# Cosformer attention with a mixture of adapters: the last six slots in three pairs, x of late outputs added by GpSimd, logits ahead of the transposes of x

## The chip, the cores and the metric

The kernel runs on one core of a Trainium2 chip. The metric is device time in microseconds (us) of one execution; lower is better. Times before and after are medians over runs on a chip.

A core has five engines that run side by side, each with its own queue of instructions in program order. TensorE (PE in the profile; PEld is its weight load) multiplies matrices and transposes by multiplying with an identity. VectorE (DVE) and ScalarE (ACT) do elementwise work and can read PSUM, where matmuls write. GpSimd (POOL) does elementwise work in SBUF and here also issues the loads. SyncE (SP) issues the stores. 16 DMA engines move data between the chip's memory and SBUF.

## The reference

Inputs q, k and v have 8 batches, 8 heads, 576 positions and 64 features. A linear attention with cosine weights comes first:

```python
theta = np.pi / 2.0 * pos / S
phi(x) = concat([relu(x) * cos(theta), relu(x) * sin(theta)])     # 128 features
kv  = einsum('bhsf,bhsd->bhfd', phi(k), v)
z   = sum(phi(k), axis=2)
num = einsum('bhsf,bhfd->bhsd', phi(q), kv)
den = einsum('bhsf,bhf->bhs', phi(q), z) + 1e-06
x   = (num / den), heads side by side: 4608 rows of 512
```

Then a mixture of adapters on x, with 8 experts of rank 16, of which each row uses the best two:

```python
logits = x @ w_gate
topk   = the two largest of a row's 8 logits
w      = softmax over these two
out    = x + sum over the two experts e of w[e] * (x @ A[e]) @ B[e]
```

## The kernel before, in words

**Tiles.** The 4608 rows of x are worked in 36 slots of 128 rows, NT in the code. Nine slots serve two batches: slots 0 to 3 of each nine belong to the first, 5 to 8 to the second, and the fifth (numbers 4, 13, 22, 31; `mixed`) holds 64 rows of each. A position is written as r * 9 + s, so a batch has nine columns s of 64 rows, and a slot takes two columns.

**Loads.** k, q and v of each batch come by one load each, nearly all issued by GpSimd, cast to bf16 on the way. Five buffers of each are used in turn: after the last scaling of one batch's k, GpSimd issues the loads of batches further on (`load_k(b + 3)`, `load_q(b + 2)`, `load_v(b + 3)`).

**Attention.** For each batch k is cut at zero and multiplied by cos and sin: `relu_k` on VectorE cuts columns in place and `scale_k` on GpSimd multiplies, two instructions for a column. Of batches 2 to 7, GpSimd does columns 0 to 6 in this way; VectorE does column 7 and ACT column 8, cut and multiplied in one instruction (`scale_k1`). `kv` on TensorE sums phi(k) x v over a batch's nine columns into the two PSUM banks `cd`, with a column of ones beside v for z, and `kv_out` copies the sums to SBUF on ACT. For a slot, `transp_q` transposes q and multiplies it by cos and sin in one matmul against a diagonal (from slot 27 on in 64x64 pieces, line 201; before that line 213), `evac_q` copies it out of PSUM on ACT with the cut at zero, `numden` multiplies it with the sums (lines 247 and 252), and `normalise` on VectorE takes the reciprocal of the denominators (line 259) and writes x to SBUF in bf16 (`xt`, line 266).

**Mixture.** `transp_x` transposes x into PSUM (`xz`, line 274), `evac_x` copies it to SBUF on VectorE (line 280). `logits` multiplies it with all experts' A and with w_gate at once, into a PSUM bank `za` (line 300). Slots are gated in groups that share a bank `za`: `gate_a` (maximum, sum, mask, scale) and `gate_b` (mask times sigmoid, and the product with x @ A, giving `zg`, line 335) run on VectorE, with the sigmoid on ACT in between (`gate_sig`, line 326). `za` has one buffer, so the next group's first logits wait for this group's `zg`. `transp_z` transposes `zg` into the other half of `xz` (line 348), and the next `evac_x` takes it along; at the end `evac_z` copies it alone. Then `delta` makes the output in one PSUM bank with two matmuls: x times the identity (`delta_x`, line 366) and `zg` times all experts' B (`delta_z`, line 371). `evac_o` copies it to SBUF on ACT as f32 (line 382, tile `osb`, 24 buffers) and `store` sends it off on SP. The outputs' banks are the two `cd`, in turn, or, while `kv` holds these, a buffer of `qd` that the q transposes use otherwise.

**Order.** The order on every engine is the order of the program, written by hand. The loop over slots n is, in this order: the copy of x transposed of slot n - 1; `normalise(n)`; q of slot n + 1 (`move_q`); logits that are "early"; some `kv`; the gates; one output or two from the list `todo`; `transp_x(n)`; `transp_z`; VectorE's share of k and the cut; GpSimd's share with the loads behind it; logits that are "late"; `numden(n + 1)`; ACT's share of k. Tables such as `early_at`, `late_at`, `gate_a_at` and `move_at` say at which n each group comes. Stores are held back until k of batch 7 has landed (line 529 and `held`). After the loop the last slots are finished by a sequence written out.

**Groups before.** Slots 0 to 32 form eleven groups of three, 33 and 34 a pair, and 35 a group of its own, with a bank from `qd`. For most groups all three logits are late ones, in the step before the first gate.

Of the kernel before, what the change touches and what calls it, by code (L numbers as in the profile page):

```python
# [13 lines left out]
NS = 9  # L14
# [5 lines left out]
def kernel(ctx, tc, q, k, v, w_gate, A, Bw, out):  # L20
# [255 lines left out]
    def evac_x(n, g=None):  # L276

        c = DCH if g is None else DCH + len(groups[g])
        xT_t[n] = t = p_xt.tile([128, DCH + 3, 128], BF16, name="xT")
        nc.vector.tensor_copy(t[:, 0:c], xz[:, 0:c * 128].rearrange("p (c s) -> p c s", c=c))  # L280
        if g is not None:
            zgT_t[g] = t[:, DCH:]

    groups = [list(range(i, i + 3)) for i in range(0, NT - 3, 3)]
    groups += [[NT - 3, NT - 2], [NT - 1]]
    group_of = {n: g for g, t in enumerate(groups) for n in t}

    def logits(n):
        g = group_of[n]
        i = n - groups[g][0]  # L290
        if i == 0:
            if g == len(groups) - 1:
                t = qd.tile([128, 512], FP32, name="zb", tag="qd")
            else:
                t = ps.tile([128, 512], FP32, name="za")
            za_t[g] = t[:, 0:3 * ZW].rearrange("p (i z) -> p i z", z=ZW)
            u_t[g] = t[:, 3 * ZW:3 * ZW + 3 * E].rearrange("p (i e) -> p i e", e=E)
        xT = xT_t.pop(n)
        for c in range(DCH):
            nc.tensor.matmul(out=za_t[g][:, i, :], lhsT=xT[:, c, :], rhs=AW[:, :, c, :],  # L300
                             start=(c == 0 and i == 0), stop=(c == DCH - 1),
                             skip_group_check=True)
# [36 lines left out]

    def zT_ps(g):  # L340
        n = len(groups[g])
        at = 512 + (256 if g == len(groups) - 1 else 0)
        return xz[:, at:at + n * 128].rearrange("p (c s) -> p c s", c=n)

    def transp_z(g):
        zg = g_t.pop(g)
        for i in range(len(groups[g])):
            nc.tensor.transpose(out=zT_ps(g)[:, i], in_=zg[:, i], identity=ident)
# [25 lines left out]
    def delta(n, own=True):  # L374
        delta_x(n, own)
        delta_z(n)

    def evac_o(n, eng="act"):
        src = osb_t[n]
        osb_t[n] = t = p_o.tile([128, DM], FP32, name="osb")  # L380
        if eng == "act":
            nc.scalar.copy(t, src)  # L382
        else:
            nc.vector.tensor_copy(t, src)
# [15 lines left out]
    def put(at, step, what):  # L400
        at.setdefault(step, []).append(what)
# [5 lines left out]
    kv_at[3] = [(1, s) for s in (5, 4, 7, 8, 6)]  # L407
    for b in range(2, B):
        first = b // 2 * NS + b % 2 * 4
        at = {2: 5, 3: 8, 4: 12, 5: 15, 6: 21, 7: 24}[b]  # L410
        for s0, s1 in ((0, 3), (3, 7)):
            put(relu_at, at, (b, s0, s1))
        for s in range(7):
            put(pool_at, at, (b, s))
        for i in range(2):
            put(dve_at, at, (b, 7, i))
            put(act_at, first - 4 + i, (b, 8, i))
        for ahead, cols in ((2, (7, 0, 1, 2)), (1, (3, 4, 5, 8, 6))):
            for s in cols:
                put(kv_at, first - ahead, (b, s))  # L420

    early_at, late_at, gate_a_at, gate_b_at, move_at = {}, {}, {}, {}, {}
    prev = 5
    for g, t in enumerate(groups[:-2]):
        tight = g > 7
        at = max(t[-1] + (1 if tight else 2), prev + 1)
        if g == 1:
            at += 1  # L430
        for n in t:
            if n + 1 == at:
                put(early_at, at, n)
            else:
# [5 lines left out]
    put(late_at, NT - 2, NT - 3)  # L440

    with tc.manual_schedule():
        for s in range(6):
            make_diag(s)
        wu = qd.tile([128, DM], FP32, name="wu", tag="qd")
        for i in range(24):
            nc.tensor.matmul(out=wu, lhsT=ones, rhs=wide, start=True, stop=True)  # L447
        for s in range(NS):
            scale_k(0, s, ("act" if s < 7 else "dve", "dve"))
            kv(0, s)  # L450
        nc.scalar.activation(warm, halfpi, AF.Sigmoid)
        for s in range(6, NS):
# [23 lines left out]
        def emit(d, own=True, eng="act"):  # L476
            delta(d, own)
            evac_o(d, eng)
            if held is None:
                store(d)  # L480
            else:
                held.append(d)

        for n in range(NT - 1):
            if n > 0:
                g = move_at.get(n - 1, (None,))[0]
                evac_x(n - 1, g)
                if g is not None:
                    todo += groups[g]
            normalise(n)  # L490
# [12 lines left out]
            for g in gate_b_at.get(n, ()):  # L503
                gate_b(g)
            now = todo[:2 if len(todo) > 3 else 1]
            del todo[:len(now)]
            for d in now:
                emit(d, n not in kv_at)
            for g in gate_a_at.get(n, ()):
                gate_sig(g)  # L510
            transp_x(n)
            for g in move_at.get(n, ()):
                transp_z(g)
            for b, s, i in dve_at.get(n, ()):
                scale_k1(b, s, i, "dve")
            for b, s0, s1 in relu_at.get(n, ()):
                relu_k(b, s0, s1)
            for b, s in pool_at.get(n, ()):
                scale_k(b, s)
                if s == 6:  # L520
# [47 lines left out]
_INS = ['q', 'k', 'v', 'moe_w_gate', 'moe_A', 'moe_B']  # L568
_OUTS = [((4608, 512), 'float32')]
# [25 lines left out]
```

## Time and profile before

| | us |
|---|---|
| median of 3 runs | 116.31 |
| lowest to highest | 116.16 to 116.43 |
| profiled execution | 116.59 |
| its span, first to last instruction and transfer | 114.8 |
| busy: TensorE / VectorE / ACT / GpSimd | 97.4 / 81.3 / 77.5 / 59.1 |

The profiled execution has 1.8 us around its span. In rows of single instructions the columns are: start, duration, engine, line, operation, output<-input with shapes, count, and in brackets idle time before it and what ended that. Rows of stages are: stage, its length, then busy time and instructions of PE, PEld, DVE, ACT and POOL, TensorE's granted clock, the DMA engines' busy share and GB/s. Rows of the chain are start, duration, engine, tile and line. Matmuls overlap: their pace is the distance of their starts, not their duration.

### The profile page before, as it was taken

To read this page: it belongs to the slowest core of one execution; us is meant where nothing else is said; L and a number is where in the kernel's file an instruction comes from. 1 tells how busy PE (TensorE), PEld (TensorE's weight loads), DVE (VectorE), ACT (ScalarE), POOL (GpSimd) and SP (SyncE) were. 2 spreads that over 40 slices of the span, in tenths; PEclk is the share of its full clock that TensorE was granted. 3 is DMA by queue.
4 is the path that set the end of the run, shared out by engine and by line. 5 is a ranking of instruction groups with operands and counts; after the bars stand their busy time and mean duration, and the time that the engine had idled before them with its cause. 6 is when DMAs were issued, how large, how long until landed. Compare 5 with 4: busy or idle time off the path is not lost.

```text
span 114.8 us, 5003 instructions
## 1 busy us (share of the span) xinstructions
PE 97.4 (85%) x2087; PEld 74.0 (65%) x2108; DVE 81.3 (71%) x288; ACT 77.5 (68%) x169; POOL 59.1 (51%) x118
## 2 busy tenths in 40 slices
PE   3998686877998999999999999999997998988710
PEld 1347466766876688777788788578786876655200
DVE  5697588559849858799666974996589448696520
ACT  5088579746845947588786964995769486795820
POOL 5991222248999995899996008959900000000000
PEclk9999999999999999999999999999999999999998
DMA  2999999999999999999999999999989335342692
GB/s 41 381 209 206 210 209 206 203 189 210 205 211 206 208 208 208 208 208 208 207 210 206 214 203 242 275 345 375 347 300 360 121 91 183 113 158 106 225 328 90
DMA packets 19670, 24.77 MB, mean 216 GB/s; under 512 B 2624, under 2 KB 14528, under 8 KB 19648
## 3 DMA queue, kind: packets, MB, share of 16 engines
q0 software_dynamic: 13856, 13.84, 72.5%
q1 hardware_dynamic: 5792, 10.62, 26.3%
q8 instruction: 16, 0.26, 0.9%
q14 instruction: 6, 0.05, 0.1%
HBM read 28.85 MB, written 9.44 MB: 334 GB/s over the span
## 4 chain that ended last, share of the span: by engine, by line
PE 45%; DMA 28%; DVE 12%; issue 4%; ACT 3%; POOL 3%; POOLq 0%; ACTq 0%
DMA k<-in_k_dram 14%; DMA v<-in_v_dram 12%; PE cd L180 10%; PE nd L252 6%; PE xz L274 6%; PE za L300 6%; PE qd L213 6%; DVE xt L266 4%; PE dx L366 3%; PE qd L201 2%; PE cd L371 2%; DVE zg L335 2%; DMA out_dram<-osb 2%; DVE xT L280 2%; ACT qpT L229 2%
## 5 line engine op out<-in xcount | busy, mean ns | idle before, releaser
L229 ACT ACTIVATE qpT<-qd 128x512 bf16<-128x512 f32 x71 | 38.6, 596 | 19.5 <-PE qd L213 14.6
L280 DVE COPY xT<-xz 128x512 bf16<-128x512 bf16 (+1 forms) x36 | 17.1, 475 | 13.5 <-PE xz L274 9.0
L266 DVE TENSOR_TENSOR xt<-nd,rden 128x512 bf16<-128x512 f32 x36 | 24.9, 691 | 1.2
L156 POOL TENSOR_SCALAR kp<-k,cos_tab 128x256 bf16<-128x256 bf16 x42 | 20.2, 480 | 10.5 <-PE cd L180 7.0
L180 PE MATMUL cd<-v,kp 64*128 64x128 bf16 x576 | 18.9, 217 | 1.4 <-DMA v<-in_v_dram 1.1
L156 POOL TENSOR_SCALAR kp<-k,sin_tab 128x256 bf16<-128x256 bf16 x42 | 20.0, 476 | 0.0
L274 PEld LDWEIGHTS <-xt 128*128 128x128 bf16 x144 | 10.2, 116 | 14.5 <-DVE xt L266 11.9
L252 PE MATMUL nd<-kvsb,qpT 128*128 128x65 bf16 (+1 forms) x320 | 17.5, 195 | 1.0 <-DVE qpT L231 0.5
L180 PEld LDWEIGHTS <-kp 64*128 64x128 bf16 x576 | 16.3, 94 | 3.1 <-issue 1.1
L274 PE MATMUL xz<-ident,xt 128*128 128x128 bf16 x144 | 14.6, 224 | 4.3 <-DVE xt L266 3.4
L213 PE MATMUL qd<-diag,q 128*64 128x128 bf16 x432 | 17.2, 222 | 0.7 <-DMA q<-in_q_dram 0.7
L213 PEld LDWEIGHTS <-q 128*64 128x64 bf16 x432 | 12.9, 109 | 2.1 <-DMA q<-in_q_dram 0.8
L382 ACT COPY osb<-cd 128x512 f32<-128x512 f32 x23 | 13.4, 594 | 1.2 <-PE cd L371 0.8
L252 PEld LDWEIGHTS <-qpT 128*128 128x128 bf16 (+1 forms) x320 | 12.6, 99 | 2.1 <-ACT qpT L229 0.7
L300 PE MATMUL za<-AW,xT 128*128 128x144 bf16 x140 | 11.4, 226 | 0.5 <-DVE zg L335 0.5
L247 PE MATMUL nd<-eps_hi,ones 128*128 128x4 bf16 x72 | 11.6, 169 | 0.0
L259 DVE RECIPROCAL rden<-nd 128x8 f32<-128x8 f32 x36 | 7.3, 203 | 5.9 <-PE nd L252 5.7
L300 PEld LDWEIGHTS <-xT 128*128 128x128 bf16 x144 | 9.3, 98 | 1.6 <-DVE xT L280 0.6
L62 POOL DMA_DIRECT2D v<-in_v_dram x8 | 6.2, 779 | 5.1 <-DMA q<-in_q_dram 4.3
L382 ACT COPY osb<-dx 128x512 f32<-128x512 f32 x12 | 6.9, 595 | 2.7 <-remote 2.7
L447 PE MATMUL wu<-wide,ones 128*128 128x512 bf16 x24 | 6.7, 448 | 2.0 <-DVE AW L115 2.0
L62 POOL DMA_DIRECT2D q<-in_q_dram x8 | 6.2, 770 | 3.4 <-DMA k<-in_k_dram 3.4
(69 smaller groups left out, 129.6 us busy)
## 6 DMA issues: line engine op xcount, KB each, us to landing
out_dram<-osb SPq DMA_DIRECT2D x32, 256.0 KB, 4.2
v<-in_v_dram POOLq DMA_DIRECT2D x8, 576.0 KB, 17.8
q<-in_q_dram POOLq DMA_DIRECT2D x8, 576.0 KB, 16.5
k<-in_k_dram POOLq DMA_DIRECT2D x7, 576.0 KB, 15.0
k0f<-in_k_dram SPq DMA_DIRECT2D x1, 1152.0 KB, 5.4
out_dram<-osb SPq DMA_DIRECT2D x8, 128.0 KB, 2.9
AW<-in_moe_A_dram POOLq DMA_DIRECT2D x1, 128.0 KB, 18.2
Ball<-in_moe_B_dram POOLq DMA_DIRECT2D x1, 128.0 KB, 16.7
```

Of the source, the lines that this page charges most:

```text
L62: eng.dma_start(out=t, in_=rows(dram, b))
L156: nc.gpsimd.tensor_scalar(out=dst, in0=src, scalar1=tab, scalar2=1.0, op0=ALU.mult, op1=ALU.mult)
L180: nc.tensor.matmul(out=kvz[par][:, g], lhsT=kp_t[b][pr, s, g], rhs=v_rhs(b, g, s, pr), start=(first and g == 0), stop=(last and g == G - 1))
L213: nc.tensor.matmul(out=t[cols, j, 2 * gi:2 * gi + 2, :], lhsT=q_b[b][:, 2 * gp + gi, s, :], rhs=diag[:, s, i], start=(j == 0 and gi == 0), ...
L229: nc.scalar.activation(t, src, AF.Relu)
L247: nc.tensor.matmul(out=nd[:, gg, D:4 * W:W], lhsT=ones, rhs=eps_hi, start=True, stop=False, skip_group_check=True)
L252: nc.tensor.matmul(out=nd[pr, gg, j * W:(j + 1) * W], lhsT=qpT[:, j, pr], rhs=kv_t[b][:, h % 2, h // 2, :], start=False, stop=(j == 3), sk ...
L266: nc.vector.tensor_tensor(out=x, in0=nd[:, :, :, 0:D], in1=rden.rearrange("p (g j) -> p g j", g=2).to_broadcast([128, 2, 4, D]), op=ALU.mult)
L274: nc.tensor.transpose(out=xz[:, c * 128:(c + 1) * 128], in_=x[:, c], identity=ident)
L280: nc.vector.tensor_copy(t[:, 0:c], xz[:, 0:c * 128].rearrange("p (c s) -> p c s", c=c))
L300: nc.tensor.matmul(out=za_t[g][:, i, :], lhsT=xT[:, c, :], rhs=AW[:, :, c, :], start=(c == 0 and i == 0), stop=(c == DCH - 1), skip_group_ ...
L382: nc.scalar.copy(t, src)
```

## The change

Six things change, mostly in the planning of the order.

- Groups: slots 0 to 29 form ten groups of three and 30 to 35 three pairs. All use the bank `za`.
- Placement of groups: the fifth to eighth groups are gated one step earlier, the eleventh too (it has only slots 30 and 31), and logits move from behind `transp_x` to the place ahead of `kv` and of `transp_x` ("early") where the tables allow it. The first logits of a group whose bank is freed only in that step stay late.
- k: GpSimd scales five columns of batch 2, seven of batch 3, eight of batches 4 and 5, and all nine of batches 6 and 7. ACT takes columns 5, 6 and 8 of batch 2 and column 8 of batches 3, 4 and 5; VectorE column 7 of batches 2 and 3. The steps at which GpSimd starts are 5, 8, 12, 17, 20, 23 where they were 5, 8, 12, 15, 21, 24. `kv` takes the columns in another order.
- Loads behind a batch's scaling come after its last column on GpSimd, whichever that is.
- Late outputs: in steps 28 to 34 (seven outputs, 22 to 28) TensorE only multiplies `zg` with B; ACT copies that to SBUF and GpSimd adds x in place (`delta_add`) before the store.
- The end: the second gate of slots 32 and 33 comes right behind the last `normalise`, outputs 33, 34 and 35 come behind the last z transposes, and VectorE copies output 34 where it copied 35.

```diff
-    groups = [list(range(i, i + 3)) for i in range(0, NT - 3, 3)]
-    groups += [[NT - 3, NT - 2], [NT - 1]]
+    groups = [list(range(i, i + 3)) for i in range(0, NT - 6, 3)]
+    groups += [[i, i + 1] for i in range(NT - 6, NT, 2)]
...
+    def delta_add(n, own=True):
+
+        if own:
+            dx = cd[dx_n[0] % 2]
+            dx_n[0] += 1
+        else:
+            dx = qd.tile([128, DM], FP32, name="dx", tag="qd")
+        g = group_of[n]
+        nc.tensor.matmul(out=dx, lhsT=zgT_t[g][:, n - groups[g][0], :], rhs=Ball,
+                         start=True, stop=True)
+        osb_t[n] = dx
+        evac_o(n)
+        t = osb_t[n]
+        nc.gpsimd.tensor_tensor(out=t, in0=t, in1=xt_t.pop(n), op=ALU.add)
...
-        at = {2: 5, 3: 8, 4: 12, 5: 15, 6: 21, 7: 24}[b]
-        for s0, s1 in ((0, 3), (3, 7)):
+        at = {2: 5, 3: 8, 4: 12, 5: 17, 6: 20, 7: 23}[b]
+        n_pool = {2: 5, 3: 7, 4: 8, 5: 8}.get(b, 9)
+        for s0, s1 in ((0, 3), (3, n_pool)):
             put(relu_at, at, (b, s0, s1))
-        for s in range(7):
+        for s in range(n_pool):
             put(pool_at, at, (b, s))
         for i in range(2):
-            put(dve_at, at, (b, 7, i))
-            put(act_at, first - 4 + i, (b, 8, i))
...
+            if n_pool <= 7:
+                put(dve_at, at, (b, 7, i))
+            if n_pool < 9:
+                put(act_at, first - 4 + i, (b, 8, i))
+            if n_pool == 5:
+                put(act_at, first - 3 + i, (b, 6, i))
+                put(act_at, first - 2, (b, 5, i))
...
-    for g, t in enumerate(groups[:-2]):
-        tight = g > 7
-        at = max(t[-1] + (1 if tight else 2), prev + 1)
+    for g, t in enumerate(groups[:-1]):
+        at = max(t[-1] + 1, prev + 1)
         if g == 1:
             at += 1
         for n in t:
-            if n + 1 == at:
-                put(early_at, at, n)
+            if t[-1] + 1 < at or (n < t[-1] and prev == at - 1):
+                put(late_at, at - 1, n)
             else:
-                put(late_at, at - 1, n)
+                put(early_at, max(n + 1, at - 1), n)
...
-                emit(d, n not in kv_at)
+                emit(d, n not in kv_at, add=n > 27)
...
-        evac_x(NT - 2)
+        evac_x(NT - 2, g10)
         normalise(NT - 1)
-        transp_z(g10)
-        logits(NT - 2)
-        evac_z(g10, [("act", 0, 3)])
+        gate_b(g11)
         todo += groups[g10]
-        for d in todo[:-3]:
+        for d in todo[:-1]:
             emit(d)
         transp_x(NT - 1)
-        gate_a(g11)
-        emit(todo[-3])
-        gate_sig(g11)
         evac_x(NT - 1)
+        logits(NT - 2)
+        transp_z(g11)
         logits(NT - 1)
-        gate_b(g11)
-        emit(todo[-2])
+        evac_z(g11, [("act", 0, 2)])
+        emit(todo[-1])
         gate_a(g12)
-        transp_z(g11)
-        evac_z(g11, [("act", 0, 2)])
         gate_sig(g12)
-        emit(todo[-1])
+        emit(NT - 4)
         gate_b(g12)
+        transp_z(g12)
+        evac_z(g12, [("dve", 0, 2)])
         emit(NT - 3)
-        transp_z(g12)
-        evac_z(g12, [("dve", 0, 1)])
-        emit(NT - 2)
-        emit(NT - 1, eng="dve")
+        emit(NT - 2, eng="dve")
+        emit(NT - 1)
```

More of the change, by code (lines that the diff above doesn't have):

```diff
@@ L291, in logits @@
         if i == 0:
[L292 to L295, printed above, removed]
+            t = ps.tile([128, 512], FP32, name="za")
             za_t[g] = t[:, 0:3 * ZW].rearrange("p (i z) -> p i z", z=ZW)
@@ L341, in zT_ps @@
         n = len(groups[g])
-        at = 512 + (256 if g == len(groups) - 1 else 0)
-        return xz[:, at:at + n * 128].rearrange("p (c s) -> p c s", c=n)
+        return xz[:, 512:512 + n * 128].rearrange("p (c s) -> p c s", c=n)
     def transp_z(g):
@@ L409 @@
         first = b // 2 * NS + b % 2 * 4
-        at = {2: 5, 3: 8, 4: 12, 5: 15, 6: 21, 7: 24}[b]
-        for s0, s1 in ((0, 3), (3, 7)):
+        at = {2: 5, 3: 8, 4: 12, 5: 17, 6: 20, 7: 23}[b]
+        n_pool = {2: 5, 3: 7, 4: 8, 5: 8}.get(b, 9)
+        for s0, s1 in ((0, 3), (3, n_pool)):
             put(relu_at, at, (b, s0, s1))
-        for s in range(7):
+        for s in range(n_pool):
             put(pool_at, at, (b, s))
         for i in range(2):
-            put(dve_at, at, (b, 7, i))
-            put(act_at, first - 4 + i, (b, 8, i))
-        for ahead, cols in ((2, (7, 0, 1, 2)), (1, (3, 4, 5, 8, 6))):
-            for s in cols:
-                put(kv_at, first - ahead, (b, s))
+            if n_pool <= 7:
[5 more added lines that the diff above has]
+                put(act_at, first - 2, (b, 5, i))
+        order = (7, 0, 1, 2, 3, 4, 8, 6, 5) if n_pool <= 7 else (0, 1, 2, 3, 4, 5, 8, 6, 7)
+        if n_pool == 9:
+            order = range(NS)
+        for j, s in enumerate(order):
+            put(kv_at, first - (2 if j < 4 else 1), (b, s))
     early_at, late_at, gate_a_at, gate_b_at, move_at = {}, {}, {}, {}, {}
     prev = 5
-    for g, t in enumerate(groups[:-2]):
-        tight = g > 7
-        at = max(t[-1] + (1 if tight else 2), prev + 1)
+    for g, t in enumerate(groups[:-1]):
+        at = max(t[-1] + 1, prev + 1)
         if g == 1:
@@ L474, with emit @@
         first_loads = persist.tile([1, 8], BF16, name="first_loads")
-        def emit(d, own=True, eng="act"):
-            delta(d, own)
-            evac_o(d, eng)
+        def emit(d, own=True, eng="act", add=False):
+            if add:
+                delta_add(d, own)
+            else:
+                delta(d, own)
+                evac_o(d, eng)
             if held is None:
@@ L519 @@
                 scale_k(b, s)
-                if s == 6:
+                if (b, s) == pool_at[n][-1]:
                     if b + 3 < B:
```

1 line of the change is left out of this document (removed).

## The prediction

> **What bounds the kernel now.** I read the page first (engine shares, the slices, the chain), then the chain in order of time, then busy time by stage, then the order of instructions on each engine where stages differ.
>
> ```profile
> PE 97.4 (85%) x2087; PEld 74.0 (65%) x2108; DVE 81.3 (71%) x288; ACT 77.5 (68%) x169; POOL 59.1 (51%) x118
> DMA  2999999999999999999999999999989335342692
> 18.82 15.56 DMA k<-in_k_dram
> 34.90 0.81 DVE k L165 x2
> ...
> 47.36:83.98 36.62, 35.32 (x760) 28.22 (x768) 27.93 (x94) 27.80 (x61) 27.64 (x58) 1.00 1.16 253
> 83.98:101.30 17.32, 16.04 (x452) 12.39 (x455) 12.48 (x43) 12.98 (x28) 0.00 (x0) 1.00 0.55 191
> ```
>
> The chain is a transfer until 34.4 us (18.82 + 15.56): the load of k for batch 3, which VectorE awaits in slot 8. From there nothing waits for loads. Between 47.36 and 83.98 us (slots 13 to 26) TensorE is busy 35.32 of 36.62 us at full clock: it is the bound, with 1.3 us of gaps. From 83.98 to 101.30 GpSimd is idle and TensorE has the same 1.3 us of gaps in half the time.
>
> I count in steps: from the start of TensorE's q transposes for one slot to the next slot's.
>
> ```profile
> 88.17 0.45 PE L201 MATMUL qd<-diag,q 64*64 64x64 bf16 x32
> 91.28 0.45 PE L201 MATMUL qd<-diag,q 64*64 64x64 bf16 x32
> 95.04 0.45 PE L201 MATMUL qd<-diag,q 64*64 64x64 bf16 x32
> ...
> 50.59 0.38 PE L371 MATMUL cd<-Ball,xT 128*128 128x512 bf16 x1
> 50.81 0.39 PE L274 MATMUL xz<-ident,xt 128*128 128x128 bf16 x4
> 51.03 0.17 PE L247 MATMUL nd<-eps_hi,ones 128*128 128x4 bf16 x1
> 51.42 0.64 PE L213 MATMUL qd<-diag,q 128*64 128x128 bf16 x16
> ```
>
> The paces, first from the starts above, then from the chain in order of time:
>
> ```profile
> 52.97 0.17 PE xz L348 x3
> 53.13 0.75 PE za L300 x12
> 54.18 0.57 PE qd L213 x16
> 54.75 1.00 PE cd L180 x32
> 57.86 1.22 PE cd L180 x40
> ```
>
> A matmul of the output pair costs 0.22 us (50.59 to 50.81), the pair 0.43, four x transposes 0.22 (to 51.03), a slot's numerators 0.39 (to 51.42). Three z transposes cost 0.17, one slot's logits 0.25 (0.75 for three), q transposes 0.57 (0.38 from slot 27), kv sums 1.00 for four columns and 1.22 for five.
>
> **The change, part by part.**
>
> *Loads and columns of k.* Batch 2 goes from seven GpSimd columns to five, so 4 scalings fewer at 0.455 apart: its three load issues move from 33.65 to about 31.9.
>
> ```profile
> 33.65 0.79 POOL L62 DMA_DIRECT2D k<-in_k_dram  x1
> 34.81 0.90 DVE L165 TENSOR_SCALAR k<-k 128x768 bf16<-128x768 bf16 x2
> 45.81 0.69 DVE L165 TENSOR_SCALAR k<-k 128x768 bf16<-128x768 bf16 x2
> ```
>
> VectorE's two relus took 0.90 us while GpSimd issued loads, 0.69 while it stood idle, and they are on the chain. The issues will be over by 34.2: **-0.2**. The Trainium skill, "SBUF — State Buffer", § Who interferes with whom, says that VectorE in a two-port mode and GpSimd shut each other out for whole instructions; the rows agree. The transfers start no earlier (the DMA row is full), and the load that is waited for was issued long before. ACT's four scalings more for batch 2 end before the wait for k at 34.4 does. Later issues move too: those after batch 4 by 0.9 (two more scalings), q of batch 7 by two steps, to about 66, still 20 us before slot 31 needs it; the stores on SP wait for k of batch 7, which stays queued behind earlier loads. Eight scalings leave VectorE and four leave ACT (slots 23 to 28); only the one that held up ACT's q copy at 86.80 is ahead of something that waits, and is counted below.
>
> A cost here: batch 6 now has 18 scalings, 8.2 us, begun behind batch 5's sixteen and a load issue, hence about 67.0 to 75.2. The relu of batch 7 comes up on VectorE at about 74.7. By the rows above it may have to wait for the port. If until 75.2, it ends near 75.9, and the x copy behind it, which needs its transposes at 75.8, moves by **+0.1**. Bounds: 0, and 1.3 (the stream, as long as it is, begun 1.2 later).
>
> *Steps 13 to 26.* Groups come one step earlier: TensorE does one output pair (0.43) and one group of z transposes (0.17) more in here. The logits ahead of the x transposes cost the same 0.25 and fill time in which TensorE would wait for x. Slot 14 gets a wait: its logits sit behind the gate of the group before, which frees the bank. Against each step's length before, by these paces: 14 +0.86 (two logits, and 0.36 for the wait); 15 -0.62 (three logits out, one in, a gap of 0.1 gone); 17 and 20 +0.67 each (two logits and z transposes in); 18 -0.33 (three logits and z transposes out, one logit and a pair in, a gap gone); 19 -0.06 (a gap); 21 -0.67 (three logits and z transposes out, one logit in); 23 +0.43 (two logits and z transposes in, less gaps); 24 -0.69 (as 21); 26 +0.17 (z transposes); the others nothing. Together **+0.4**. With no gap filled it is +0.9 (0.43 + 0.17 + 0.3 for the wait), with every gap gone -0.7 (0.6 less 1.3).
>
> *Steps 27 to 34.* Each of the seven late outputs drops its 0.22 us matmul; step 30 emits one output where two were. But two other loops set a floor.
>
> ```profile
> 86.80 1.09 ACT L229 ACTIVATE qpT<-qd 128x512 bf16<-128x512 f32 x2 [0.19 <-ACT kp L151]
> 93.34 0.65 ACT L188 CAST kvsb<-cd 128x260 bf16<-128x260 f32 x2 [0.42 <-PE cd L180]
> 99.93 1.08 ACT L229 ACTIVATE qpT<-qd 128x512 bf16<-128x512 f32 x2 [0.86 <-PE qd L201]
> 101.07 0.30 PE L252 MATMUL nd<-kvsb,qpT 128*128 128x65 bf16 x4
> 101.30 0.45 PE L201 MATMUL qd<-diag,q 64*64 64x64 bf16 x32
> 101.86 1.08 ACT L229 ACTIVATE qpT<-qd 128x512 bf16<-128x512 f32 x2 [0.26 <-PE qd L201]
> ...
> 101.66 0.69 DVE L266 TENSOR_TENSOR xt<-nd,rden 128x512 bf16<-128x512 f32 x1
> 102.47 0.56 DVE L335 TENSOR_TENSOR zg<-za,em 128x384 bf16<-128x384 f32 x1
> 103.08 0.42 PE L300 MATMUL za<-AW,xT 128*128 128x144 bf16 x4 [0.27 <-DVE zg L335]
> 103.85 0.21 DVE L259 RECIPROCAL rden<-nd 128x8 f32<-128x8 f32 x1 [0.50 <-PE nd L252]
> 104.09 0.69 DVE L266 TENSOR_TENSOR xt<-nd,rden 128x512 bf16<-128x512 f32 x1
> ```
>
> First, q transposes to ACT to numerators: 99.93 to 101.86, 1.92 us. Second, a step whose logits wait for the gate of the same step: 101.66 to 104.09, 2.43 us. After: step 27 1.92 (was 1.93); 28 1.92 (was 2.26: ACT's k scaling stood before the q copy at 86.80 and is gone); 29 2.91 (was 3.11); 30 3.28 (was 3.76: 0.66 less work, 0.2 back, since ACT's 0.65 us copy of the kv sums has 0.47 of cover left); 31 2.42 (was 1.92, the wait for the gate); 32 1.93 (was 2.42, one logit later removed); 33 2.50 (was 1.92, the same wait); and to the last reciprocal 2.15 (was 103.85 - 101.30 = 2.55). Sum 19.03 against 19.87: **-0.8**. Step 31 holds up numerators and the next reciprocal behind the logits; that is in the 2.42. Bounds: the dropped matmuls hidden, +0.0; no new wait, -1.4.
>
> *The add.* It isn't on TensorE's path: the output goes PSUM to SBUF on ACT as before and only its store waits. The price isn't in the trace.
>
> ```profile
> 72.42 0.48 POOL L156 TENSOR_SCALAR kp<-k,sin_tab 128x256 bf16<-128x256 bf16 x1
> 72.88 0.48 POOL L156 TENSOR_SCALAR kp<-k,cos_tab 128x256 bf16<-128x256 bf16 x1
> 72.99 0.41 DVE L280 COPY xT<-xz 128x512 bf16<-128x512 bf16 x1
> 100.97 0.42 DVE L280 COPY xT<-xz 128x512 bf16<-128x512 bf16 x1
> ```
>
> A scaling of 256 elements takes 0.48 us. Twice the elements makes 0.93; five times the bytes (two inputs, f32) makes 2.4. I take 1.4, nearer the instruction of the same engine. The cover: adds come one per 2.0 to 3.3 us from about 87.2, and the last store issue comes at 110.0, behind eight store issues of about 0.6 (four took 2.56, quoted below); so the seven adds must end by 105.2, 18.0 us for seven, 2.6 us each. Behind a late add waits SP's whole queue. VectorE's copies from PSUM took 0.41 beside a busy GpSimd and 0.42 beside an idle one, so the adds don't slow them. The Trainium skill, "GPSIMD Engine Reference", § 3.1, gives an add of 2048 f32 as 4497 ns, by which an estimate for 512 is 1.1 us; its § 2.1 adds about 6 us once for the first call of a freshly loaded kernel. No run here shows that yet, and by it the sum would be the same.
>
> *The end.* The final sequence before:
>
> ```profile
> 105.72 0.58 ACT L382 COPY osb<-cd 128x512 f32<-128x512 f32 x1 [0.44 <-DMA out_dram<-osb]
> 106.20 0.19 ACT L326 ACTIVATE za<-tg 128x16 f32<-128x16 f32 x1
> 108.58 2.56 SPq L395 DMA_DIRECT2D out_dram<-osb  x4
> 109.63 0.69 DVE L384 COPY osb<-cd 128x512 f32<-128x512 f32 x1 [0.66 <-PE cd L371]
> ```
>
> (The wait at 105.72 is not for a store: the output's matmuls end just then.) ACT's sigmoid at 106.20 stood behind that copy, then two gates in a row. The change gates slots 32 and 33 in the loop's rhythm, with their sigmoid done before slot 35's x. From the last x (t = 0, 104.09 before): zg at 0.81, x transposes 0.75, x copy 1.20, logits 1.28 and 1.67, gate to 2.75, sigmoid 3.02 (behind one output copy), zg 3.45, z transposes 3.92, z copy 4.23, output 34 at 4.69, output 35 at 5.50 because its bank is output 33's, which now comes behind the z transposes; ACT's copy ends at 6.49 and SP issues the last store at 6.51. Before: 108.58 + 2.56 less one issue of about 0.6, less 104.09: 6.45. **0.0** within 0.1, bounds -0.4 (the bank free in time) and +0.5.
>
> **The sum.** -0.2 + 0.1 + 0.4 - 0.8 + 0.0 = -0.5 us in the profiled execution, 114.8 of span in 116.59; the median of the runs is 116.31, 0.3 below, and the change is taken from that: 115.8.
>
> **Rivals.** (1) The gaps fill better: the +0.4 of steps 13 to 26 vanishes and goes to -0.2, all else as forecast: 115.2. For it: 1.3 us of gaps; against: I could fill few by hand. (2) Nothing measurable: steps 31 and 33 wait 0.2 longer each: 116.2. (3) Slower, by the port: the relu of batch 7 is shut out by GpSimd's stream. It decides from a stall of 0.6 us in all, that is, when batch 6's stream ends after 75.7; with a stall of 1.3, 117.0. For it: the stream is back to back, 0.455 apart with 0.48 each, and batches 5, 6 and 7 now follow without a pause; against: 0.5 us is all that is left of it when the relu comes. (4) The add is dear: at 3.0 us the last stores go 3.0 later, 118.8. Only the byte bound comes near. By the skill's 6 us and 2.4 us an add together, the adds end 4.8 late, 120.6; with 1.4 us they end at 103.0 and cost nothing.
>
> **How the numbers follow.** Forecast 0.50 (115.4 to 116.1), (1) 0.15, (2) 0.10, (3) 0.18, (4) 0.07. A measurement can tell about 0.2%, 0.23 us, from no change. Faster: 0.15 and nearly all of the forecast, 0.62; same: (2) and the forecast's edge, 0.13; slower 0.25. Range 114.9 to 116.8: below, a twentieth; above, (4) and the worse third of (3).
>
> **What would show it.** The relus at slot 8 at 0.69; the q transposes that stand at 83.98 near 0.3 later; 0.8 us less from there to the last reciprocal, with steps 31 and 33 near 2.4 showing TensorE's logits released by zg; relus of batch 7 longer than 0.75 would speak for (3); adds above 2.6 us, or SP waiting for GpSimd after 105, for (4). The prediction is wrong if those q transposes come after 84.7, or if the last x isn't earlier than 104.09.

## The result: 116.89 us, slower by half a per cent

| | before | after |
|---|---|---|
| median, us (9 runs each) | 116.29 | 116.89 |
| lowest to highest | 116.10 to 116.43 | 116.74 to 117.36 |
| profiled execution / its span | 116.59 / 114.8 | 117.36 / 115.6 |

The ratio is 1.0053, with a 95% interval of 1.0037 to 1.0069: slower, by more than the 0.2% that can be told from no change, and 0.1 us above the predicted range (114.9 to 116.8, with 115.8 as the forecast). The execution profiled for the changed kernel was the longest of its nine. A second profile of the same kernel (`after_again`) has 116.71 and a span of 114.9; where the two differ, both are given.

The page of the changed kernel: engine shares, GpSimd's slices, and the new operation's group (busy us, mean ns, idle before it and what ended that).

```profile
PE 100.4 (87%) x2101; PEld 74.4 (64%) x2101; DVE 79.9 (69%) x280; ACT 76.9 (67%) x168; POOL 71.2 (62%) x133
POOL 5992222247988994999179989989910435544000
L387 POOL TENSOR_TENSOR osb<-osb,xt 128x512 f32<-128x512 f32 x7 | 8.1, 1158 | 13.3 <-ACT osb L393 13.3
```

GpSimd now works until 105.6 us. An add takes 1.16 us, and GpSimd waits for ACT before the adds (13.3 us in all). The stages that the prediction used, each from one start of q transposes to another, first of `after`, then of `after_again`:

```profile
47.10:84.98 37.88, 37.16 (x776) 28.69 (x772) 27.28 (x88) 27.77 (x60) 33.07 (x70) 1.00 1.15 255
84.98:102.26 17.28, 15.55 (x448) 11.78 (x445) 12.92 (x45) 12.03 (x27) 6.11 (x6) 1.00 0.45 157
```

```profile
47.04:84.35 37.31, 36.92 (x778) 28.62 (x774) 27.21 (x88) 27.71 (x60) 32.93 (x70) 1.00 1.14 251
84.35:101.62 17.27, 15.54 (x447) 11.77 (x445) 12.91 (x45) 12.01 (x27) 6.10 (x6) 1.00 0.50 175
```

Slot 8, the relus of batch 7 and the end in `after`, on VectorE, TensorE, ACT and SP:

```profile
34.36 0.29 DVE L153 TENSOR_SCALAR kp<-k,cos_tab 128x256 bf16<-128x256 bf16 x1 [1.12 <-DMA k<-in_k_dram]
34.76 0.69 DVE L165 TENSOR_SCALAR k<-k 128x768 bf16<-128x768 bf16 x2
...
74.84 1.28 DVE L165 TENSOR_SCALAR k<-k 128x768 bf16<-128x768 bf16 x2
...
104.62 0.69 DVE L266 TENSOR_TENSOR xt<-nd,rden 128x512 bf16<-128x512 f32 x1
...
108.21 0.42 DVE L332 TENSOR_TENSOR zg<-za,em 128x256 bf16<-128x256 f32 x1
```

```profile
106.41 0.41 PE L297 MATMUL za<-AW,xT 128*128 128x144 bf16 x4
...
108.69 0.28 PE L344 MATMUL xz<-ident,zg 128*128 128x128 bf16 x2 [1.00 <-DVE zg L332]
110.08 0.38 PE L362 MATMUL cd<-xt,ident 128*128 128x512 bf16 x1 [0.24 <-ACT osb L393]
...
110.71 0.59 ACT L393 COPY osb<-cd 128x512 f32<-128x512 f32 x1 [0.68 <-PE cd L367]
...
109.14 2.79 SPq L406 DMA_DIRECT2D out_dram<-osb  x4
```

Term by term, in us. "Undisturbed" sets `after_again` against the profile of before, and in steps 13 to 26 against a kernel that equals the one before up to slot 27 (`b_add`, below), for a reason that the section on the prediction gives.

| term | forecast | profile to profile | undisturbed |
|---|---|---|---|
| slot 8, from k's landing to slot 13's q transposes (43.54 - 34.41; 43.28 - 34.36) | -0.2 | -0.21 | -0.21 |
| steps 13 to 26, relu of batch 7 in it | +0.5 | 37.88 - 36.62 = +1.26 | 37.31 - 36.39 = +0.92 |
| steps 27 to the last x (104.09 - 83.98; 104.62 - 84.98) | -0.8 | 19.64 - 20.11 = -0.47 | -0.47 |
| last x to the end of the span (114.79 - 104.09; 115.56 - 104.62) | 0.0 | 10.94 - 10.70 = +0.24 | +0.24 |
| sum | -0.5 | +0.82 | +0.48 |

By the medians the change made +0.60. The execution of `after_again` in the last column lay 0.18 below the median of its runs.

### The profile page after: what moved, and what is told of

It is laid out like the page before. It is cut to its first block, busy times and chain, and to the rows that moved or that the text cites. A ratio compares the mean times of both kernels' runs of the same rounds, so it can differ in the third digit from the quotient of the medians.

```text
span 115.6 us, 5017 instructions
## 1 busy us (share of the span) xinstructions
PE 100.4 (87%) x2101; PEld 74.4 (64%) x2101; DVE 79.9 (69%) x280; ACT 76.9 (67%) x168; POOL 71.2 (62%) x133
## 4 chain that ended last, share of the span: by engine, by line
PE 49%; DMA 25%; DVE 13%; issue 3%; POOL 3%; ACT 3%; POOLq 0%; ACTq 0%
DMA k<-in_k_dram 14%; DMA v<-in_v_dram 12%; PE cd L180 10%; PE za L297 8%; PE qd L213 7%; PE nd L252 6%; DVE xt L266 5%; PE xz L274 5%; DVE zg L332 3%; PE dx L362 2%; PE cd L362 2%; DVE xT L280 2%; PE cd L367 2%; PE qd L201 2%; PE xz L344 2%
## 5 line engine op out<-in xcount | busy, mean ns | idle before, releaser
L280 DVE COPY xT<-xz 128x512 bf16<-128x512 bf16 (+2 forms) x36 | 17.3, 479 | 15.2 <-PE xz L344 8.3
L156 POOL TENSOR_SCALAR kp<-k,cos_tab 128x256 bf16<-128x256 bf16 x46 | 22.6, 490 | 7.2 <-DVE k L165 6.4
L156 POOL TENSOR_SCALAR kp<-k,sin_tab 128x256 bf16<-128x256 bf16 x46 | 21.9, 476 | 0.0
L387 POOL TENSOR_TENSOR osb<-osb,xt 128x512 f32<-128x512 f32 x7 | 8.1, 1158 | 13.3 <-ACT osb L393 13.3
L393 ACT COPY osb<-cd 128x512 f32<-128x512 f32 x24 | 13.9, 594 | 2.3 <-PE cd L367 2.2
L297 PE MATMUL za<-AW,xT 128*128 128x144 bf16 x144 | 12.8, 227 | 1.0 <-DVE zg L332 0.7
L464 PE MATMUL wu<-wide,ones 128*128 128x512 bf16 x24 | 8.3, 525 | 2.0 <-DVE AW L115 2.0
L393 ACT COPY osb<-dx 128x512 f32<-128x512 f32 x11 | 6.4, 594 | 3.8 <-PE dx L367 3.0
```

Of the source, the lines that this page charges most:

```text
L156: nc.gpsimd.tensor_scalar(out=dst, in0=src, scalar1=tab, scalar2=1.0, op0=ALU.mult, op1=ALU.mult)
```

## Experiments

Three theories for the loss: **A**, the new placement of logits and groups costs; **B**, the pairs and the new end cost; **C**, GpSimd's longer shares of k and VectorE shut each other out. Names with b_ are the kernel before with one part of the change; names with a_ are the changed kernel with one part undone or moved. Each ratio is to the kernel before on the same chip, with its 95% interval.

### One part of the change alone

`b_logits`: the placement.

```diff
-        tight = g > 7
-        at = max(t[-1] + (1 if tight else 2), prev + 1)
+        at = max(t[-1] + 1, prev + 1)
...
-            if n + 1 == at:
-                put(early_at, at, n)
-            else:
+            if t[-1] + 1 < at or (n < t[-1] and prev == at - 1):
                 put(late_at, at - 1, n)
+            else:
+                put(early_at, max(n + 1, at - 1), n)
```

> The kernel before with only the placement of the changed one (logits ahead of kv and of the x transposes, the fifth to eighth groups gated one step earlier), groups, k, add and end as before. Theory A (this placement is what costs: TensorE does more in steps 13 to 26, loses about 0.1 us at each change from logits to kv, ACT gets two outputs and a k scaling in one step): slower by 0.5 to 0.9 us, 116.8 to 117.2, q transposes of slot 28 at 84.5 or later. Theory B (the pairs and the new end cost): within 0.2 of before. Theory C (GpSimd and VectorE block each other because of the longer k share): within 0.2 of before.

Measured: 116.48, ratio 1.0021 (1.0004 to 1.0039). Steps 13 to 26 take 37.28, as long as in the whole change; from there to the last x 19.43 (84.54 to 103.97), 0.7 less than before. Placement costs 0.9 in one stage and has 0.7 back in the next.

`b_end`: groups and end (the groups' lines of the diff shown ahead of the prediction and its part after the loop, nothing else).

```diff
-    groups = [list(range(i, i + 3)) for i in range(0, NT - 3, 3)]
-    groups += [[NT - 3, NT - 2], [NT - 1]]
+    groups = [list(range(i, i + 3)) for i in range(0, NT - 6, 3)]
+    groups += [[i, i + 1] for i in range(NT - 6, NT, 2)]
...
```

> The kernel before with only the groups of two and the sequence after the loop of the changed kernel; placement up to slot 29 as before. Theory A: within 0.2 of before (steps 31 and 33 +0.5 and +0.4, steps 32 and the last -0.9, the end +0.2). Theory B: slower by 0.5 or more, 116.8, of which 0.3 or more behind the last x. Theory C: as A.

Measured: 116.64, ratio 1.0037 (1.0024 to 1.0051). From slot 28's q transposes to the last x 20.24 (+0.13), from there to the end 10.95 (+0.25). B costs by itself.

`b_k`: the shares of k, with their order in `kv`.

```diff
-        at = {2: 5, 3: 8, 4: 12, 5: 15, 6: 21, 7: 24}[b]
+        at = {2: 5, 3: 8, 4: 12, 5: 17, 6: 20, 7: 23}[b]
+        n_pool = {2: 5, 3: 7, 4: 8, 5: 8}.get(b, 9)
...
```

> The kernel before with only the changed shares of k (and their steps and order in kv). Theory A: a little faster, 116.0, by the relus of slot 8 (-0.2) and ACT's k scalings gone from slots 27 and 28 (-0.3), less the relu of batch 7 that waits. Theory B: as A. Theory C: slower by 0.4 or more, with relus on VectorE above 1.0 us for the pair at two or more batches.

Measured: 117.32, ratio 1.0113 (1.0075 to 1.0151), the dearest part. Batch 7's relus on VectorE, TensorE's x transposes behind them, and GpSimd's last two scalings of batch 6:

```profile
74.51 1.70 DVE L165 TENSOR_SCALAR k<-k 128x768 bf16<-128x768 bf16 x2
76.13 0.41 DVE L280 COPY xT<-xz 128x512 bf16<-128x512 bf16 x1
77.44 0.43 PE L274 MATMUL xz<-ident,xt 128*128 128x128 bf16 x4 [1.56 <-DVE xt L266]
...
74.61 0.47 POOL L156 TENSOR_SCALAR kp<-k,cos_tab 128x256 bf16<-128x256 bf16 x1
75.06 0.47 POOL L156 TENSOR_SCALAR kp<-k,sin_tab 128x256 bf16<-128x256 bf16 x1
```

Two relus that took 0.69 beside an idle GpSimd take 1.70 here. GpSimd's stream ends at 75.53 (75.06 + 0.47) and the relus at 76.21, 0.68 later: they ran only once the stream was over, and TensorE stood still for 1.56. (Batch 6's relus, from 65.99 to 67.50, were slow too, beside two scalings and a load issue; the two steps there, 20 and 21, are as long as before.) By the Trainium skill, "SBUF — State Buffer", § Who interferes with whom, whoever issues first keeps the shared ports for one instruction. These rows go further: VectorE did not get in where one GpSimd instruction followed the other without a pause (at 74.61 and 75.06).

In this profiled execution (118.78, the longest of its runs) TensorE's clock fell after that pause. Stages: length, busy times, then the granted clock.

```profile
72.82:76.00 3.18, 3.06 (x53) 1.83 (x50) 3.11 (x7) 2.64 (x7) 2.71 (x6) 1.00 1.12 304
77.40:80.00 2.60, 2.56 (x29) 2.52 (x29) 0.62 (x1) 0.00 (x0) 2.60 (x7) 0.56 1.04 388
80.00:82.00 2.00, 2.00 (x51) 1.74 (x48) 1.50 (x8) 1.08 (x2) 2.00 (x6) 0.72 1.04 383
```

`b_add`: the add.

```diff
-                emit(d, n not in kv_at)
+                emit(d, n not in kv_at, add=n > 27)
```

> The kernel before with only the add of x on GpSimd for the outputs of steps 28 to 34 (eight outputs here). Theories A and B: faster by 0.3 to 0.7 us, 115.6 to 116.0, all of it between the q transposes of slot 28 and the last x. Theory C: no gain, 116.3, since the adds slow VectorE's copies or the stores.

Measured: 116.00, ratio 0.9978 (0.9964 to 0.9992). Eight matmuls of 0.22 us (this kernel has eight outputs in these steps) are gone from TensorE and 0.2 us from the time: from slot 28's q transposes to the last x 19.88 (83.70 to 103.58) instead of 20.11.

### One part taken out of the change

`a_nologits`: the placement of before.

```diff
-        at = max(t[-1] + 1, prev + 1)
+        tight = g > 7
+        at = max(t[-1] + (1 if tight else 2), prev + 1)
...
```

> The changed kernel with the placement of before for all groups (logits behind the x transposes, groups gated as late as before); k shares, add, pairs and end stay. Theory A (the placement costs): faster than before by 0.3 to 0.6 us, 115.7 to 116.0. Theory B (the pairs and the new end cost): still slower than before, 116.7 or more. Theory C (GpSimd and VectorE block each other): 116.7 or more.

Measured: 117.17, ratio 1.0087 (1.0070 to 1.0104), worse than the whole change. Its relus of batch 7 start at 74.48 and take 1.70, with TensorE idle for 1.56, as in `b_k`. In the change they come at 74.84, because the steps ahead are longer, and wait only 0.6. The placement thus pays for part of C: the parts do not add up singly (-0.20, +0.28, +0.44 and +1.12 make 1.64, the whole 0.6).

`a_noend`: groups and end of before.

```diff
-    groups = [list(range(i, i + 3)) for i in range(0, NT - 6, 3)]
-    groups += [[i, i + 1] for i in range(NT - 6, NT, 2)]
+    groups = [list(range(i, i + 3)) for i in range(0, NT - 3, 3)]
+    groups += [[NT - 3, NT - 2], [NT - 1]]
...
```

> The changed kernel with the groups and the end of before; placement by its own rule up to the eleventh group, k shares and add stay. Theory A: within 0.3 of the changed kernel, 116.6 to 117.2. Theory B: 0.5 or more faster than the changed kernel, 116.3 or less. Theory C: as A.

Measured: 116.12, ratio 1.0001 (0.9986 to 1.0017): 0.77 less than the change. Logits and q transposes of the changed kernel (`after_again`), and q transposes of `a_noend`:

```profile
94.74 0.58 PE L201 MATMUL qd<-diag,q 64*64 64x64 bf16 x32
96.52 0.42 PE L297 MATMUL za<-AW,xT 128*128 128x144 bf16 x4 [0.27 <-DVE zg L332]
97.18 0.44 PE L201 MATMUL qd<-diag,q 64*64 64x64 bf16 x32
99.11 0.45 PE L201 MATMUL qd<-diag,q 64*64 64x64 bf16 x32
101.62 0.45 PE L201 MATMUL qd<-diag,q 64*64 64x64 bf16 x32
```

```profile
94.89 0.57 PE L201 MATMUL qd<-diag,q 64*64 64x64 bf16 x32
96.92 0.45 PE L201 MATMUL qd<-diag,q 64*64 64x64 bf16 x32
98.85 0.45 PE L201 MATMUL qd<-diag,q 64*64 64x64 bf16 x32
100.81 0.45 PE L201 MATMUL qd<-diag,q 64*64 64x64 bf16 x32
```

With pairs, steps 31 and 33 take 2.44 and 2.51, since their logits wait for the gate of the same step; with threes they take 2.03 and 1.96. To the last x that makes 19.64 against 19.20, and the end is 10.94 against 10.68.

`a_nok`: the shares of k of before.

```diff
-        at = {2: 5, 3: 8, 4: 12, 5: 17, 6: 20, 7: 23}[b]
+        at = {2: 5, 3: 8, 4: 12, 5: 15, 6: 21, 7: 24}[b]
...
```

> The changed kernel with the shares of k of before. Theories A and B: slower than the changed kernel by 0.2 to 0.4, 117.1 to 117.3. Theory C: faster by 0.3 or more, 116.6 or less.

Measured: 116.76, ratio 1.0053 (1.0037 to 1.0069). Within the change, the new shares are worth next to nothing either way. By the traces of `after_again` and `a_nok` they gain 0.15 up to slot 13 and 0.18 in step 25 (2.62 for 2.80), and lose 0.25 in step 28 (2.20 for 1.96), 0.08 in step 26, and 0.07 in step 24, where the relus wait.

`a_noadd`: no add.

```diff
-                emit(d, n not in kv_at, add=n > 27)
+                emit(d, n not in kv_at, add=False)
```

> The changed kernel with both matmuls for every output and no add on GpSimd. Theories A and B: slower than the changed kernel by 0.3 to 0.6, 117.2 to 117.5. Theory C: the same or faster.

Measured: 117.14, ratio 1.0092 (1.0071 to 1.0112). The add saves 0.25 by the medians, 0.45 by the ratios, and 0.44 by the traces from slot 28's q transposes to the last x (20.08 without it, 19.64 with it). The end is as long either way (10.93 and 10.94).

### Moving one thing

`a_kvfirst`: the early logits behind the sums of k and v.

```diff
-            for t in early_at.get(n, ()):
-                logits(t)
...
+            for t in early_at.get(n, ()):
+                logits(t)
```

> The changed kernel with the early logits behind kv instead of ahead of it, in the steps that have both (17, 20, 21, 26, 29, 30). Theory A (TensorE loses about 0.1 us where the kv sums follow logits directly): 0.3 to 0.6 us faster than the changed kernel, 116.3 to 116.6, eight logits take 0.50 in place of 0.61. Rival: the order of the two costs nothing or the same 0.1 comes at the other change: within 0.15 of the changed kernel.

Measured: 116.13, ratio 0.9990 (0.9979 to 1.0001), 0.76 less than the change from an exchange of two neighbours on one engine. The chain (start, us, what): eight logits in slot 26 of the kernel before, then slot 17 of `after_again`, then the same slot of `a_kvfirst`:

```profile
83.24 0.50 PE za L300 x8
```

```profile
57.10 0.63 PE qd L213 x16
57.73 0.61 PE za L297 x8
58.34 1.22 PE cd L180 x40
59.56 0.32 PE dx L362
59.88 0.22 PE dx L367
```

```profile
57.10 0.63 PE qd L213 x16
57.72 1.22 PE cd L180 x40
58.95 0.61 PE za L297 x8
59.55 0.21 PE dx L362
```

Eight logits had 0.50 in the kernel before, where they stood between other matmuls of 128 rows and columns; here they have 0.61, and the output matmul behind the sums has 0.32 instead of 0.22. q transposes are 128*64, the sums of k and v 64*128, logits and outputs 128*128: at each such change of shape in these rows about 0.1 us goes. In the change the shape changes three times (q, logits, sums, output), before and in `a_kvfirst` twice. The steps 17, 20, 21, 26, 29 and 30, which have early logits and sums, are shorter by 0.11, 0.10, 0.11, 0.11, 0.10 and 0.18; step 24, whose relus now wait longer, has 0.07 of it back. The Trainium skill, "TensorEngine Tiling (Array Packing)", § Key Properties, says that a change of tiling mode drains TensorE. The rows agree, and give the price in this kernel.

`a_out33`: output 33 ahead of the last z transposes, so that its bank is free for output 35.

```diff
+        emit(NT - 3)
         transp_z(g12)
         evac_z(g12, [("dve", 0, 2)])
-        emit(NT - 3)
```

> The changed kernel with output 33 made ahead of the last z transposes, where TensorE stood idle for 1.0 us, so that its bank is free for output 35 in time. Theory A (output 35 waits for its bank at the end): 0.3 to 0.5 us faster than the changed kernel, 116.4 to 116.6, output 35's copy ends 0.4 earlier after the last x. Rival (the end is set by the gate's chain and by SP's issues): within 0.15, 116.75 to 117.05.

Measured: 116.58, ratio 1.0031 (1.0019 to 1.0043), 0.3 less than the change. The wait for ACT ahead of output 35 (0.24 at 110.08 above) is gone, and the end takes 10.72, as in the kernel before (10.70).

`a_relu24`: cut and scalings of batch 7 one slot later.

```diff
-        at = {2: 5, 3: 8, 4: 12, 5: 17, 6: 20, 7: 23}[b]
+        at = {2: 5, 3: 8, 4: 12, 5: 17, 6: 20, 7: 24}[b]
```

> The changed kernel with batch 7's relu and GpSimd's share one step later (24 in place of 23), when batch 6's stream of scalings has ended. If the stream shuts VectorE's relus out until its end: the pair takes 0.75 in place of 1.28 us, and the kernel is 0.1 to 0.4 faster, 116.5 to 116.8. If the relus were only slower as they are longer: 1.2 to 1.3 us again, no change.

Measured: 116.78, ratio 1.0050 (1.0038 to 1.0062). The relus take 0.83 instead of 1.28, at 77.83, and step 24 takes 1.97 instead of 2.05; 0.1 us in the time, within the intervals.

`b_poolmax`: the kernel before without relus; GpSimd's own instruction cuts at zero as its second operation (the tables are not negative, so the outputs are the same).

```diff
-            nc.gpsimd.tensor_scalar(out=dst, in0=src, scalar1=tab, scalar2=1.0,
-                                    op0=ALU.mult, op1=ALU.mult)
+            nc.gpsimd.tensor_scalar(out=dst, in0=src, scalar1=tab, scalar2=0.0,
+                                    op0=ALU.mult, op1=ALU.max)
...
-        for s0, s1 in ((0, 3), (3, 7)):
-            put(relu_at, at, (b, s0, s1))
```

> The kernel before without the relus on VectorE: GpSimd's scaling multiplies by cos or sin and cuts at zero in its second operation, where it multiplied by 1 (cos and sin are not negative). If GpSimd's cut costs as much as its second multiplication: scalings stay 0.455 apart, VectorE's slot 8 is free 0.5 to 0.8 us sooner, 115.5 to 116.0. If it is dearer (0.6 us or more each): kv waits for GpSimd, 117 or more.

Measured: 153.54, ratio 1.32 (1.3155 to 1.3245).

```profile
L156 POOL TENSOR_SCALAR kp<-k,cos_tab 128x256 bf16<-128x256 bf16 x42 | 47.9, 1140 | 0.1
```

The scaling takes 1.14 us instead of 0.48, and GpSimd becomes the bound (61% of the chain, where it had 3%). The relus can't be got rid of in this way.

### Do the costs add up?

`noend_kvfirst`: `a_noend` with the early logits behind the sums (the loop over `kv_at` stands where the dots are).

```diff
-            for t in early_at.get(n, ()):
-                logits(t)
...
+            for t in early_at.get(n, ()):
+                logits(t)
```

> The changed kernel with the groups of three and the end of before, and with the early logits behind the kv sums. If the two costs are separate, 0.77 (groups and end, 116.89 to 116.12) and 0.76 (logits behind kv, 116.89 to 116.13) come off together: 115.4, ratio near 0.993. If both runs removed the same idle time, it stays at 116.0 to 116.1.

Measured: 115.25, ratio 0.9920 (0.9907 to 0.9933). They are separate costs.

`noend_kv_r24`: the same, with batch 7 one slot later.

```diff
-        at = {2: 5, 3: 8, 4: 12, 5: 17, 6: 20, 7: 23}[b]
+        at = {2: 5, 3: 8, 4: 12, 5: 17, 6: 20, 7: 24}[b]
```

> As noend_kvfirst, and the relus and GpSimd scalings of batch 7 one slot later (24 instead of 23). If the relus behind GpSimd's stream still cost in that kernel, 0.1 to 0.3 less than noend_kvfirst: 115.1 to 115.3. If the earlier steps now run ahead of GpSimd, the stream ends no earlier against them and a later slot gains the same or more; if the relu comes off the path anyway, the same as noend_kvfirst.

Measured: 115.11, ratio 0.9901 (0.9886 to 0.9916), the fastest; but the 0.14 to the kernel above is within the intervals, and the two profiled executions have the same span, 113.47. So the later slot has no gain here that can be told from nothing. Stages, relus and last x:

```profile
47.10:84.00 36.90, 36.52 (x778) 28.72 (x774) 26.72 (x88) 27.95 (x60) 30.48 (x65) 1.00 1.16 254
84.00:99.94 15.94, 14.78 (x447) 11.66 (x446) 12.14 (x44) 11.84 (x25) 8.23 (x11) 1.00 0.53 188
...
77.60 0.83 DVE L165 TENSOR_SCALAR k<-k 128x768 bf16<-128x768 bf16 x2
...
102.78 0.70 DVE xt L266
```

Against the kernel before: slot 8 -0.2, steps 13 to 26 +0.5 (36.90 to 36.39), to the last x -1.3 (18.78 to 20.11), the end 0.0 (10.69 to 10.70). That is -1.0, with -1.08 measured.

`a_kv_out33`: the edits of `a_kvfirst` and `a_out33` together, as shown there.

> The changed kernel with two moves: the early logits behind the kv sums, and output 33 ahead of the last z transposes. Separate costs: 116.13 less 0.3 (116.89 to 116.58 for output 33 alone) = 115.8. One and the same: 116.1.

Measured: 115.89, ratio 0.9972 (0.9961 to 0.9983). Nearer to the separate costs (115.8).

`after_again`: the changed kernel once more, without an edit.

> The changed kernel once more, nothing altered. The same ratio to the kernel before, 1.0053 within 0.002. If the q copy of slot 28 is late again (step 28 at 2.2 us, not 1.92), it belongs to the order of the instructions and not to that one execution; the 0.5 us stall at the first 64x64 transposes of slot 27 should not come back.

Measured: 116.89, ratio 1.0064 (1.0047 to 1.0082). Step 28 takes 2.21 as in `after`. Step 26 took 4.17 in `after` and takes 3.67 here: a pause in TensorE's 64x64 transposes in `after` (0.52 from one start to the next, 0.33 of it idle from 81.41 on), with nothing to wait for, did not come back. It is no single case: the profiled executions of `a_noadd` (0.58), `a_relu24` (0.34) and `a_out33` (0.17) pause behind the same transpose, and each was the longest of its kernel's runs. Its cause stays open.

## Why the prediction was wrong

The sum was -0.5, the change made +0.6. Three terms were mis-sized, all to the same side: steps 13 to 26 by 0.4, steps 27 to 34 by 0.4, the end by 0.2.

**Steps 13 to 26: +0.5 forecast with the relu, +0.92 measured.** The step that failed is "together +0.4". Most of its parts were near, by the starts in `after_again`: 14 +0.85 (forecast +0.86), 15 -0.65 (-0.62), 17 +0.69 (+0.67), 18 -0.35 (-0.33), 23 +0.40 (+0.43), 24 -0.63 with the relu in it (-0.59). Missed were step 19, +0.16 for -0.06, in which ACT has two output copies and a scaling of k ahead of the q copy (it starts 0.65 after the transposes, 0.52 in `b_add`); 20 and 21, +0.76 for +0.67 and -0.55 for -0.67, and 26, +0.28 for +0.17: 0.1 each, the change of shape of `a_kvfirst`, which the paces of single blocks left out. Step 17 pays it too, and came near its forecast because as much went elsewhere in it. Step 26 is counted from the 3.39 that it takes in `b_end` and `b_k` (3.42 in `b_add`). The profile of before has 3.65 there, a stall like that of `after`; it is most of the 0.3 by which that execution lay above its median, and why the comparison of the two profiles has to be mended in the last column of the table.

**The "1.3 us of gaps" was for the most part missing records.** On it rested rival 1 and the lower bound of -0.7. Busy time counts the records that a trace has. The output matmuls of line 371 in this stage of before, and then the whole stage and that line in `b_add`, which runs the same code there:

```profile
47.36:83.98 36.62, 3.41 (x9) 1.58 (x16) 1.00 1.16 253
```

```profile
47.31:83.70 36.39, 36.28 (x771) 28.16 (x767) 27.93 (x94) 27.81 (x61) 27.58 (x58) 1.00 1.16 253
47.31:83.70 36.39, 6.06 (x16) 1.58 (x16) 1.00 1.16 253
```

The trace of before has 9 matmuls of this line with 16 weight loads, and 760 matmuls in the stage where 771 ran. The missing eleven look like idle time; `b_add`, which has them, is busy 36.28 of its 36.39 us. The rows that the prediction quotes had the sign in them: fewer matmuls than weight loads, x760 and x768 in the stage, x2087 and x2108 in the whole execution (in `b_add` x2100 and x2100).

Busy time doesn't measure the room in a stage either. In step 15 of `b_add`, then of `after_again`:

```profile
52.17 0.38 PE L371 MATMUL cd<-Ball,xT 128*128 128x512 bf16 x1
52.51 0.41 PE L274 MATMUL xz<-ident,xt 128*128 128x128 bf16 x4
```

```profile
52.98 0.38 PE L367 MATMUL cd<-Ball,xT 128*128 128x512 bf16 x1
53.20 0.39 PE L274 MATMUL xz<-ident,xt 128*128 128x128 bf16 x4
```

The x transposes start 0.34 behind the output matmul in the first, 0.22, its pace, in the second. The 0.12 between is a gap, and the matmul's recorded 0.38 covers it. The forecast took 0.45 of such small gaps in steps 15, 18 and 23, and these came out as forecast, so work moved in did fill gaps. The measured +0.92 lies at the range's end "no gap filled", +0.9, by coincidence: gaps were filled, and 0.1 each in steps 20, 21 and 26 and 0.2 in step 19, which no part of the forecast had, came on top.

**Steps 27 to 34: -0.84 forecast, -0.47 measured.** The mechanism held: steps 31 to 33 took 2.44, 1.93 and 2.51 (2.42, 1.93, 2.50 forecast), released by `zg` as said. Step 28 took 2.21, not 1.92: its q copy on ACT starts 0.84 after the transposes (86.31 to 87.15), not 0.59 as in step 27 (84.35 to 84.94).

```profile
86.37 0.23 ACT L323 ACTIVATE za<-tg 128x24 f32<-128x24 f32 x1
87.15 1.08 ACT L229 ACTIVATE qpT<-qd 128x512 bf16<-128x512 f32 x2 [0.55 <-PE cd L382]
```

The view puts the wait down to the output matmul behind the transposes (86.69 to 87.08). That can't be all: in the last step of `a_noend` the same matmul follows the transposes at the same distance (100.81 to 101.19), and the copy starts after 0.55.

```profile
101.19 0.39 PE L386 MATMUL cd<-Ball,xT 128*128 128x512 bf16 x1
101.36 1.09 ACT L229 ACTIVATE qpT<-qd 128x512 bf16<-128x512 f32 x2 [0.30 <-PE qd L201]
```

The late copy comes back in every kernel here that has the new shares of k and the new placement both, and is not in those with one of them: `a_nok` 1.95, `a_nologits` 1.97, `b_logits` 1.96, `b_k` 1.97. Its cause stays open. Step 29 took 0.09 more by the change of shape.

**The end: 0.0 forecast, +0.24 measured, above its +0.1 and inside its bound of +0.5.** From the last x, `zg`, x transposes, x copy and the first logits came at 0.81, 0.75, 1.20 and 1.29 in `after` (0.81, 0.75, 1.20, 1.28 forecast). The two z transposes ahead of the second logits were counted at nothing: these come at 1.79 for 1.67, and the last z copy at 4.39 for 4.23. That did not reach the end, since output 35 starts at 5.46 (5.50). What failed is behind it: ACT's copy starts at 6.09 where I had 5.90. I took about the pace of outputs in a row, 0.43, for a pair with nothing behind it, which takes the 0.22 to its second matmul and that one's whole 0.38. The price of its bank was in the forecast and left standing; `a_out33`, without it, ends 0.22 sooner after its last x, and `a_noend` shows that the old end was 0.26 better.

**What held.** Slot 8 at -0.2, with relus at 0.69. The add hidden: 1.16 us (1.4 taken); by the Trainium skill, "GPSIMD Engine Reference", § 3.1, the estimate was 1.1, and of the 6 us of its § 2.1 for a first call the trace shows nothing (the seven adds take 8.1 in all, the first 1.16 like the rest). The last add ends at 105.61, later than the 105.2 allowed for it, but the end is no longer for it: `a_noadd`, without adds, has 10.93. Rival 3 named the right mechanism and the place, and its price by itself (`b_k`, +1.12 for 1.3); inside the change 0.6 of wait was left of it, of which `a_relu24` finds 0.07 in step 24, near the +0.1 of the forecast. None of the rivals had what decided: the changes of shape, ACT's late q copies in steps 19 and 28, and the last output's pair.

## What to carry to other kernels

Before a stage is called one with gaps, compare the counts of matmuls and weight loads in it, or a second profile: missing records look like idle time. The recorded duration of a matmul can also cover a wait, so look for room in the distances of starts, step by step. Count changes of the matmuls' shape in a moved step as work, and for the last instruction of a chain take its full duration, not the pace of a row. A change of several parts is worth taking apart: here the old groups and end and one exchange of neighbours turn a loss of 0.6 us into a gain of 0.9 (`noend_kvfirst`).

## What the runs showed of the hardware

- A change of the shape of matmuls (128*64, 64*128, 128*128) costs about 0.1 us in this kernel; an exchange of two blocks took 0.7 us off six steps and 0.76 off the time.
- Two relus on VectorE took 1.70 us instead of 0.69 beside GpSimd's scalings without a pause, and ended only after these (`b_k`, and the same in `a_nologits`).
- GpSimd's `tensor_scalar` of 256 bf16 takes 0.48 us as multiply and multiply, 1.14 as multiply and maximum.
- After 1.56 us of pause TensorE had a granted clock of 0.56 over 2.6 us and 0.72 over the next 2.0 in the profiled execution of `b_k`, and 1.00 after the same pause in that of `a_nologits`. What decides it stays open.
